# Attention scores from four 64x64 products on the quarters of the array instead of one 128x128 product with two heads on its diagonal

## Chip, core and metric

The kernel runs on one core of one Trainium2 chip. The metric is device time in microseconds (us), the median of several executions; lower is better. The kernel before takes 703.58 us (three runs, 703.25 to 704.31).

A core has five engines that run their own instruction queues in order and wait for each other through semaphores. PE (TensorE) multiplies matrices: a weight load (LDWEIGHTS, listed as PEld) puts the stationary operand, up to 128 rows by 128 columns, into the array, and the matmul streams the moving operand's columns through it into PSUM. DVE (VectorE), ACT (ScalarE) and POOL (GpSimd) do element-wise work, SP issues DMAs.

## The reference

Local attention with summaries, then a feed-forward layer. Batch 4, 8 heads, 768 tokens, head size 64; model width 512, inner width 2048. Each query sees the keys nearer than 16 positions, and 24 summaries of 32 keys each (the maximum over a block's keys; the mean over its values):

```python
k_sum = k.reshape(B, H, nb, block, D).max(axis=3)
v_sum = v.reshape(B, H, nb, block, D).mean(axis=3)
scores_l = scale * np.matmul(q, k.transpose(0, 1, 3, 2))      # kept where |query - key| < 16
scores_s = scale * np.einsum('bhsd,bhnd->bhsn', q, k_sum) + np.log(block)
a = softmax(concatenate([scores_l_m, scores_s]))
x = np.matmul(a, concatenate([v, v_sum]))                     # heads side by side: 3072 x 512
h = x @ w_in
g = np.where(h >= 1, h, np.where(h <= -1, 0.0, (h + 1) ** 2 / 4))
return g @ w_out
```

## The kernel before

**Tiling.** The 3072 tokens are cut in 8 chunks of 384 (half a sequence). A chunk's attention is done for 4 pairs of heads; a pair has 6 query blocks of 64 queries, and each block sees a window of 96 keys plus the 24 summaries: KA = 120 columns. The feed-forward of a chunk has 16 steps of 128 inner columns.

**Attention of one pair.** `scores` (L196) makes the scores: for each query block one fp32 matmul with `q_t[:, blk, :]` as the stationary operand, 128 x 128. It holds the two heads of the pair on its diagonal (head 0 in rows and columns 0 to 63, head 1 in 64 to 127) and zeros elsewhere, so that the product with the 128 x 120 keys (both heads' 64 rows under each other) gives the 64 queries of head 0 in the upper partitions and those of head 1 in the lower ones. Three blocks make one PSUM tile `s_ps`, so a pair has two score tiles, j = 0 for blocks 0 to 2 and j = 1 for blocks 3 to 5. DVE scales and masks a tile into `e` (L204) and takes its maxima `nm` (L208). `exps` (L211) is ACT's exponential, `norms` (L219) divides by the sums (`den`; DVE L221, L222, then POOL L223), `transposes` (L225) turns the probabilities on PE into `t_ps` and ACT copies them to `pt` (L230), `values` (L233) multiplies them with the values: 12 matmuls a pair, each 120 rows by 64 columns, head 0 into the upper and head 1 into the lower half of `o_ps`. `mean_vals` (L191) transposes the summaries of the values.

**Feed-forward.** Weights arrive as float64 words and are split in two halves of fp32r; x and the gated g are split too, so each product is three. `ff1` (L253) is 12 matmuls of 384 columns into `h` (L259; two PSUM buffers), `gate` (L263) makes g on ACT, DVE (L268, L269), ACT and POOL; when L269 has read `h`, its buffer is free for the next `ff1` but one. `ff2` (L276) is 9 matmuls of 512 columns into three accumulators `acc` (L283).

**Weights.** Each of 16 pairs of weight pieces is converted once, during the first chunks, in three steps: `convert_top` (letter a: DVE L101, L103), `convert_low` (b: ACT L110, DVE L111), `convert_split` (c: ACT L116, POOL L117).

**Order.** The program is written as steps of one letter: S scores, E exps, N norms, T transposes, A values, F ff1, G gate, H ff2, a b c conversion. For the first two chunks' attention and the first chunk's feed-forward the order is a table (`FIRST_CHUNK`, L39); from then on one step of the next chunk's attention is put between F and H of each feed-forward step, four such steps to a pair (S E N; values in; T; A). A scheduler in the tile framework may still move independent instructions past each other within an engine's queue. All of an engine's work is one queue in that order. PSUM has six buffers for `s_ps`, `t_ps`, `vs_ps`, `o_ps` and `acc`, and two for `h`.

An fp32 matmul is carried out as two passes, each with its own weight load, so the trace has two MATMUL records for one matmul of the program; the fp32r products of the feed-forward have one.

Of the kernel before, what the change touches and what calls it, by code (L numbers as in the profile page):

```python
# [8 lines left out]
F32 = mybir.dt.float32  # L9
# [31 lines left out]
w2 E011 a0 T000 N011 K03 E010 T001 R02 S020 b0 A00 N010 S021 E020 w1 Z01 T010 E021 R03 N021 N020 T011 A01 a1  # L41
w3 Y02 S030 E030 Z02 S031 a2 T021 T020 E031 N031 Y03 b1 k10 Z03 A02 w5 T031 N030 T030 A03 c0 b2 c2 R10 w4 F00
S100 G00 k11 c1 S101 E101 E100 F01 a3 N101 G01 b3 N100 F02 R11 a4 b4 w6 H00 a5 v10 G02 c3 b5 F03 c4 T100 F04
T101 S111 Z10 w7 A10 F05 a6 H01 G03 S110 G04 b6 c5 w8 H02 w9 E111 v11 E110 a7 N110 T110 k12 Z11 R12 G05 N111
b7 H03 a8 F06 T111 A11 we wa c6 b8 wb G06 H04 H05 F07 c7 a9 b9 c8 aa G07 ba F08 S121 c9 H06 E121 S120 wc v12
F09 F0a ac G08 wd k13 R13 ca bc E120 Z12 H07 H08 N121 G09 N120 ab bb G0a H09 ad bd F0b wf ae cb cd v13 F0c Z13
S131 T120 T121 H0a G0b F0e be ce S130 A12 E130 N130 cc af G0c F0d H0b H0c E131 bf cf T130 N131 F0f T131 G0d
A13 H0d G0f G0e
# [7 lines left out]
def fused_kernel(ctx: ExitStack, tc: tile.TileContext, q2, kT, kwin, vT, vwin, w_in, w_out, mask, ident, out):  # L56
# [12 lines left out]
    mask_sb = const.tile([P, NT + 2, KA], F32, name="mask_sb")  # L69
# [37 lines left out]
    def convert_low(i):  # L107
        # the low word, rounded, gives the last 3 bits and the carry
        w, low = converting[i]
        nc.scalar.mul(out=low, in_=low.bitcast(U32), mul=2.0 ** -29)  # L110
        nc.vector.tensor_tensor(out=w, in0=w, in1=low, op=ALU.add)  # L111
# [19 lines left out]
    # what of the first chunk lies in the weights' rooms  # L131
# [64 lines left out]
    def scores(c, p, j):  # L196
        q_t, k_t = ins[c, p]
        s_ps = ps.tile([P, 512], F32, tag="ps", name=f"s_ps{c}_{p}_{j}")
        for t in range(NT):
            blk = NT * j + t  # L200
            nc.tensor.matmul(s_ps[:, t * KA:(t + 1) * KA], q_t[:, blk, :], k_t[:, blk, :], start=True, stop=True)  # L201
        e = att.tile([P, NT, KA], F32, tag=f"e{j}", name=f"e{c}_{p}_{j}", bufs=E_BUFS)
        at = c % NHALF + j
        nc.vector.scalar_tensor_tensor(  # L204
            out=e, in0=s_ps[:, :NT * KA].rearrange("p (t n) -> p t n", n=KA), scalar=1.0 / math.sqrt(D),
            in1=mask_sb[:, at:at + NT], op0=ALU.mult, op1=ALU.add)
        nm = att.tile([P, NT], F32, tag=f"nm{j}", name=f"nm{c}_{p}_{j}")
        nc.vector.tensor_reduce(out=nm, in_=e, axis=AX.X, op=ALU.max, negate=True)  # L208
        sm[c, p, j] = (e, nm)
# [23 lines left out]
    def values(c, p):  # L233
        v_t = vts[c, p]
        o_ps = ps.tile([P, 512], F32, tag="ps", name=f"o_ps{c}_{p}")
        for blk in range(NB):
            for j in range(2):
# [3 lines left out]
                    pt[c, p, blk // NT][:KA, (blk % NT) * P + j * QB:(blk % NT) * P + (j + 1) * QB],  # L241
# [21 lines left out]
    def gate(c, f):  # L263
        h_ps = hs[c, f]
        # g = max(h, min(t, 1) * t) with t = relu((h + 1) / 2)
# [29 lines left out]
    def load_constants():  # L295
        nc.sync.dma_start(out=mask_sb, in_=mask)
        nc.sync.dma_start(out=ident_sb, in_=ident)
# [101 lines left out]
```

## Time and profile before

| | |
|---|---|
| time, median of three runs | 703.58 us (703.25 to 704.31) |
| span of the profiled execution | 703.5 us, mean granted TensorE clock 0.975 |
| PE busy | 660.8 us (94%), 4064 matmul records |
| PEld busy | 591.2 us (84%) |
| DVE, ACT, POOL busy | 362.4, 336.4, 237.3 us |
| matmuls into h / acc / s_ps / t_ps / o_ps | 1536 / 1152 / 384 / 192 / 768 records |
| DMA | 69.06 MB, mean 98 GB/s |

In the timeline a row is `start us, length us, engine, line, operation, output<-inputs, shape, count`, and after it in brackets the idle time of the engine before it and what ended it. Consecutive like instructions are merged into one row with their count, and its length is then from the first one's start to the last one's end. Matmuls overlap: one's end is modelled some 0.2 us behind the start of the next, so rates are read from starts.

### The profile page before, as it was taken

The page shows a single profiled execution, that of the slowest core. Times are in us where ns is not written, and L with a number is a line of the kernel's source. Part 1 is how long each engine was busy: PE and PEld are TensorE (multiplying, and loading weights), DVE is VectorE, ACT ScalarE, POOL GpSimd, SP SyncE. Part 2 cuts the span into 40 slices and gives each one's busy share as a digit, 9 for nine tenths or more (in the row PEclk, how much of TensorE's full clock was granted, in tenths as well). Part 3 has the DMA queues.
Part 4 walks back from the last instruction along what each step waited for, and adds up shares of the span by engine and source line. Part 5 has one row for each costly group of instructions (what it writes and reads, how often), then busy time and mean ns, then how long its engine had stood idle before and what let it go on. Part 6 is the DMA issues. An engine that isn't in the chain of part 4 may idle for free.

```text
span 703.5 us, 10733 instructions
## 1 busy us (share of the span) xinstructions
PE 660.8 (94%) x4064; PEld 591.2 (84%) x4064; DVE 362.4 (52%) x671; ACT 336.4 (48%) x833; POOL 237.3 (34%) x222
## 2 busy tenths in 40 slices
PE   4858768799999999999999999999999999999997
PEld 3747667689889998989899898989899998989996
DVE  6689999956443444335444554336434443332222
ACT  4777758554444534434444544435444544433222
POOL 1336775752323232223323232223323232222221
PEclk9888988899999999999999999999999999999999
DMA  9999410136111322116212322216212320001001
GB/s 295 370 370 355 151 58 1 48 93 222 61 47 59 129 83 61 61 26 227 65 45 61 121 91 61 55 28 235 62 44 61 106 61 18 1 1 45 1 1 45
DMA packets 31379, 69.06 MB, mean 98 GB/s; under 512 B 2912, under 2 KB 11232, under 8 KB 31328
## 3 DMA queue, kind: packets, MB, share of 16 engines
q1 hardware_dynamic: 31328, 68.38, 29.9%
q8 instruction: 32, 0.52, 0.3%
q14 instruction: 19, 0.16, 0.1%
HBM read 62.07 MB, written 6.29 MB: 97 GB/s over the span
## 4 chain that ended last, share of the span: by engine, by line
PE 82%; DVE 11%; issue 3%; ACT 2%; DMA 1%; SPq 0%; POOL 0%; DVEq 0%; ACTq 0%
PE acc L283 35%; PE h L259 35%; PE s_ps L201 6%; PE o_ps L238 3%; DVE w L103 3%; PE t_ps L228 3%; DVE w L101 2%; DVE w L111 2%; DVE t L268 2%; DMA vraw<-in_vT 1%; DVE t L269 1%; ACT raw L99 1%; DVE e L204 0%; DVE nm L208 0%; PE vs_ps L193 0%
## 5 line engine op out<-in xcount | busy, mean ns | idle before, releaser
L259 PE MATMUL h<-xhi,halves 128*128 128x384 f32 x1024 | 291.6, 346 | 21.6 <-DVE t L269 20.0
L273 POOL TENSOR_TENSOR glo<-t,ghi 128x384 fp32r<-128x384 f32 x128 | 135.3, 1057 | 385.2 <-PE acc L283 187.6
L283 PE MATMUL acc<-halves,ghi 128*128 128x512 f32 x768 | 240.0, 393 | 0.0
L268 DVE SCALAR_TENSOR_TENSOR t<-t 128x384 f32<-128x384 f32 x128 | 87.0, 679 | 277.3 <-ACT t L267 277.0
L259 PEld LDWEIGHTS h<-xhi,halves 128*128 128x128 f32 x1024 | 192.2, 193 | 28.6 <-issue 17.9
L259 PE MATMUL h<-xlo,halves 128*128 128x384 f32 x512 | 175.6, 343 | 0.3 <-DVE xlo L247 0.3
L267 ACT ACTIVATE t<-h,ones_half 128x384 f32<-128x384 f32 x128 | 74.2, 581 | 211.0 <-PE h L259 211.0
L283 PEld LDWEIGHTS acc<-halves,ghi 128*128 128x128 f32 x768 | 145.3, 189 | 27.2
L283 PE MATMUL acc<-halves,glo 128*128 128x512 f32 x384 | 160.5, 418 | 0.7 <-POOL glo L273 0.7
L272 ACT CAST ghi<-t 128x384 fp32r<-128x384 f32 x128 | 65.7, 513 | 110.2 <-DVE t L269 110.1
L259 PEld LDWEIGHTS h<-xlo,halves 128*128 128x128 f32 x512 | 98.7, 193 | 5.4 <-DVE xlo L247 0.7
L283 PEld LDWEIGHTS acc<-halves,glo 128*128 128x128 f32 x384 | 72.8, 190 | 16.6 <-POOL glo L273 1.6
L215 ACT ACTIVATE e<-e,nm 128x120 f32<-128x120 f32 x192 | 73.5, 384 | 11.0 <-DVE nm L208 10.9
L269 DVE TENSOR_TENSOR t<-h,t 128x384 f32<-128x384 f32 x128 | 70.9, 554 | 3.0
L223 POOL TENSOR_TENSOR e<-e,den 128x360 f32<-128x360 f32 x64 | 55.1, 865 | 50.4 <-DVE den L222 36.7
L201 PE MATMUL s_ps<-k,q 128*128 128x120 f32 x360 | 50.2, 291 | 7.2 <-DVE k L163 5.4
L201 PEld LDWEIGHTS s_ps<-k,q 128*128 128x128 f32 x360 | 48.9, 207 | 8.2 <-issue 5.4
L117 POOL TENSOR_TENSOR halves<-w,halves 128x1024 fp32r<-128x1024 f32 x16 | 45.1, 2827 | 15.0 <-ACT halves L116 15.0
L204 DVE SCALAR_TENSOR_TENSOR e<-s_ps,mask_sb 128x360 f32<-128x360 f32 x64 | 33.6, 525 | 5.7 <-PE s_ps L201 5.5
L215 ACT ACTIVATION_READ_ACCUMULATOR e<-e,nm 128x1 f32 x192 | 35.9, 187 | 0.0
L208 DVE TENSOR_REDUCE nm<-e 128x3 f32<-128x360 f32 x64 | 33.4, 522 | 0.8
L238 PEld LDWEIGHTS o_ps<-pt,v 120*64 120x64 f32 x720 | 24.4, 141 | 10.9 <-issue 6.6
(50 smaller groups left out, 408.6 us busy)
## 6 DMA issues: line engine op xcount, KB each, us to landing
q<-in_q SPq DMA_DIRECT2D x30, 384.0 KB, 4.5
k<-in_kwin SPq DMA_DIRECT2D x28, 360.0 KB, 3.5
v<-in_vwin SPq DMA_DIRECT2D x30, 288.0 KB, 2.9
raw<-in_w_in SPq DMA_DIRECT2D x16, 512.0 KB, 9.9
raw<-in_w_out SPq DMA_DIRECT2D x16, 512.0 KB, 10.1
out<-o SPq DMA_DIRECT2D x24, 256.0 KB, 2.1
kraw<-in_kT SPq DMA_DIRECT2D x13, 384.0 KB, 3.8
vraw<-in_vT SPq DMA_DIRECT2D x13, 384.0 KB, 3.5
```

The costliest lines, as they stand in the source:

```text
L117: nc.gpsimd.tensor_tensor(out=halves[:, 1], in0=w.bitcast(F32), in1=halves[:, 0].bitcast(F32), op=ALU.subtract)
L201: nc.tensor.matmul(s_ps[:, t * KA:(t + 1) * KA], q_t[:, blk, :], k_t[:, blk, :], start=True, stop=True)
L215: nc.scalar.activation(out=e[:, t, :], in_=e[:, t, :], func=AF.Exp, bias=nm[:, t:t + 1], scale=1.0, accum_out=den[:, t:t + 1])
L223: nc.gpsimd.tensor_tensor(out=e, in0=e, in1=den.unsqueeze(2).broadcast_to([P, NT, KA]), op=ALU.mult)
L238: nc.tensor.matmul(o_ps[j * D:(j + 1) * D, blk * QB:(blk + 1) * QB], v_t[:KA, blk, j * D:(j + 1) * D], pt[c, p, blk // NT][:KA, (blk % NT) ...
L259: nc.tensor.matmul(h_ps[:, :T], weight["win", f][w][:, k * P:(k + 1) * P], x, start=(n == 0), stop=(n == 3 * NK - 1))
L267: nc.scalar.activation(out=t_sb, in_=h_ps[:, :T], func=AF.Relu, bias=ones_half, scale=0.5)
L268: nc.vector.scalar_tensor_tensor(out=t_sb, in0=t_sb, scalar=1.0, in1=t_sb, op0=ALU.min, op1=ALU.mult)
L269: nc.vector.tensor_tensor(out=t_sb, in0=h_ps[:, :T], in1=t_sb, op=ALU.max)
L272: nc.scalar.copy(out=hi, in_=t_sb)
L273: nc.gpsimd.tensor_tensor(out=lo, in0=t_sb, in1=hi.bitcast(F32), op=ALU.subtract)
L283: nc.tensor.matmul(acc[c][i], a[:, rows], weight["wout", f][w], start=(f == 0 and n == 0), stop=(f == NF - 1 and n == 2))
```

## The change

The scores are made from quarters of the array. For each block and each head a matmul of its own takes 64 rows of q and k (that head's) and 64 columns: the stationary operand is the 64 x 64 block of `q_t` on the diagonal, the moving operand that head's 64 rows of keys. Head j sits in the array's rows 64j to 64j+63; the even block of a couple (i = 0) in columns 0 to 63, the odd one (i = 1) in columns 64 to 127. So four matmuls, two heads by two blocks, cover the four quarters. What is loaded from memory is the same: `q_t` still has its zeros, which are now not read.

A score tile is now one head with all six blocks of the chunk, two blocks above each other, three couples side by side. Both tiles of a pair are made in one step (`S00` in place of `S000` and `S001`), and the table of the first chunks loses the second S of each pair. `values` reads the probabilities of head j from `pt` j. The mask has five kinds of blocks before and four columns of them after, since the upper and the lower partitions take different ones: it comes in by two DMAs of 64 partitions instead of one of 128.

```diff
-    def scores(c, p, j):
+    def scores(c, p):
         q_t, k_t = ins[c, p]
-        s_ps = ps.tile([P, 512], F32, tag="ps", name=f"s_ps{c}_{p}_{j}")
+        s_ps = [ps.tile([P, 512], F32, tag="ps", name=f"s_ps{c}_{p}_{j}") for j in range(2)]
         for t in range(NT):
-            blk = NT * j + t
-            nc.tensor.matmul(s_ps[:, t * KA:(t + 1) * KA], q_t[:, blk, :], k_t[:, blk, :], start=True, stop=True)
+            for j in range(2):
+                rows = slice(j * D, (j + 1) * D)
+                for i in range(2):
+                    blk = 2 * t + i
+                    nc.tensor.matmul(s_ps[j][i * QB:(i + 1) * QB, t * KA:(t + 1) * KA],
+                                     q_t[rows, blk, rows], k_t[rows, blk, :], start=True, stop=True)
...
-        at = c % NHALF + j
+        for j in range(2):
+            at = c % NHALF
...
-                    pt[c, p, blk // NT][:KA, (blk % NT) * P + j * QB:(blk % NT) * P + (j + 1) * QB],
+                    pt[c, p, j][:KA, blk * QB:(blk + 1) * QB],
...
-        nc.sync.dma_start(out=mask_sb, in_=mask)
+        for i in range(2):
+            rows = slice(i * QB, (i + 1) * QB)
+            nc.sync.dma_start(out=mask_sb[rows], in_=mask[rows, i:i + NT + 1])
...
-            do(f"S{c}{p}0 E{c}{p}0 N{c}{p}0 S{c}{p}1 E{c}{p}1 N{c}{p}1")
+            do(f"S{c}{p} E{c}{p}0 N{c}{p}0 E{c}{p}1 N{c}{p}1")
```

The table of the first chunks, its first row as an example:

```diff
-k00 m k01 v00 k02 K01 v01 R00 K00 w0 k03 S000 v02 R01 v03 E000 S001 E001 Y00 N001 N000 Y01 S010 Z00 S011 K02
+k00 m k01 v00 k02 K01 v01 R00 K00 w0 k03 S00 v02 R01 v03 E000 E001 Y00 N001 N000 Y01 S01 Z00 K02 w2 E011 a0
```

Two places of the engines' queues. First PE, at the first scores that lie in the steady alternation of feed-forward and attention (chunk 2, pair 0; in a name like s_ps_0_1 the numbers are the pair and the tile, the last number only tells instances apart; "x3" is three matmuls). Before:

```order
L259 MATMUL h_0_1335<-xhi_3_1306,halves_437 128x384
L201 MATMUL s_ps_0_0_1365<-k_0_1358,q_0_1360 128x120 x3
L201 MATMUL s_ps_0_1_1380<-k_0_1358,q_0_1360 128x120 x3
L283 MATMUL acc_0_557<-halves_1254,glo_14_1332 128x512
L283 MATMUL acc_0_557<-halves_1254,ghi_14_1331 128x512 x2
```

The same place now:

```order
L265 MATMUL h_0_1384<-xhi_3_1355,halves_462 128x384
L205 MATMUL s_ps_0_0_1414<-k_0_1407,q_0_1409 64x120 x2
L205 MATMUL s_ps_0_1_1415<-k_0_1407,q_0_1409 64x120 x2
...
L289 MATMUL acc_0_588<-halves_1303,glo_14_1381 128x512
L289 MATMUL acc_0_588<-halves_1303,ghi_14_1380 128x512 x2
```

Six matmuls have become twelve, in the order head 0 with two blocks, head 1 with two blocks, three times (the rows left out repeat the two above them twice); what stands before and behind them is the same.

Second DVE, where the last weights are converted (t_11 and t_12 are the gates of steps 11 and 12 of the first chunk, e_3 the scores of chunk 1, pair 3, and w the conversions; the gate's second row, which reads h, frees a buffer of h). Before:

```order
L204 SCALAR_TENSOR_TENSOR e_3_1_1119<-s_ps_3_1_1115,mask_sb 128x360
L111 ISA w_1066<-raw_990,w_1066 128x2048
L101 TENSOR_SCALAR w_1088<-raw_823 128x1024
L208 TENSOR_REDUCE nm_3_1_1121<-e_3_1_1119 128x3
L103 SCALAR_TENSOR_TENSOR w_1088<-raw_823,w_1088 128x1024
L268 SCALAR_TENSOR_TENSOR t_11_1144<-t_11_1144 128x384
L111 ISA w_1088<-raw_823,w_1088 128x2048
L269 TENSOR_TENSOR t_11_1144<-h_11_1071,t_11_1144 128x384
L101 TENSOR_SCALAR w_1206<-raw_1084 128x1024
L103 SCALAR_TENSOR_TENSOR w_1206<-raw_1084,w_1206 128x1024
L268 SCALAR_TENSOR_TENSOR t_12_1209<-t_12_1209 128x384
L269 TENSOR_TENSOR t_12_1209<-h_12_1099,t_12_1209 128x384
```

Now:

```order
L274 SCALAR_TENSOR_TENSOR t_11_1201<-t_11_1201 128x384
L100 TENSOR_SCALAR w_1255<-raw_1127 128x1024
L275 TENSOR_TENSOR t_11_1201<-h_11_1114,t_11_1201 128x384
L102 SCALAR_TENSOR_TENSOR w_1255<-raw_1127,w_1255 128x1024
L210 SCALAR_TENSOR_TENSOR e_3_0_1172<-s_ps_3_0_1158,mask_sb 128x360
L210 SCALAR_TENSOR_TENSOR e_3_1_1176<-s_ps_3_1_1159,mask_sb 128x360
L214 TENSOR_REDUCE nm_3_0_1174<-e_3_0_1172 128x3
L214 TENSOR_REDUCE nm_3_1_1178<-e_3_1_1176 128x3
L274 SCALAR_TENSOR_TENSOR t_12_1258<-t_12_1258 128x384
L110 ISA w_1255<-raw_1127,w_1255 128x2048
L227 TENSOR_SCALAR den_3_0_1244<-den_3_0_1244 128x3
L275 TENSOR_TENSOR t_12_1258<-h_12_1142,t_12_1258 128x384
```

Up to the gate of step 10 the queue has done the same set of work in both. One score tile (e and nm) that stood ahead of the gate of step 11 now stands behind it, and the last conversion's L110 (L111 before), which stood behind the gate of step 12, now stands ahead of it, together with the other score tile. On PE the matmuls that make the last two of chunk 1's `s_ps` blocks stood behind the ff1 of step 14 and now stand ahead of it.

More of the change, by code (lines that the diff above doesn't have):

```diff
@@ L39 @@
 FIRST_CHUNK = """
-k00 m k01 v00 k02 K01 v01 R00 K00 w0 k03 S000 v02 R01 v03 E000 S001 E001 Y00 N001 N000 Y01 S010 Z00 S011 K02
[L41 to L48, printed above, removed]
+k00 m k01 v00 k02 K01 v01 R00 K00 w0 k03 S00 v02 R01 v03 E000 E001 Y00 N001 N000 Y01 S01 Z00 K02 w2 E011 a0
+T000 N011 K03 E010 T001 R02 S02 b0 A00 N010 E020 w1 Z01 T010 E021 R03 N021 N020 T011 A01 a1 w3 Y02 S03 E030
+Z02 a2 T021 T020 E031 N031 Y03 b1 k10 Z03 A02 w5 T031 N030 T030 A03 c0 b2 c2 R10 w4 F00 S10 G00 k11 c1 E101
+E100 F01 a3 N101 G01 b3 N100 F02 R11 a4 b4 w6 H00 a5 v10 G02 c3 b5 F03 c4 T100 F04 T101 S11 Z10 w7 A10 F05 a6
+H01 G03 G04 b6 c5 w8 H02 w9 E111 v11 E110 a7 N110 T110 k12 Z11 R12 G05 N111 b7 H03 a8 F06 T111 A11 we wa c6 b8
+wb G06 H04 H05 F07 c7 a9 b9 c8 aa G07 ba F08 S12 c9 H06 E121 wc v12 F09 F0a ac G08 wd k13 R13 ca bc E120 Z12
+H07 H08 N121 G09 N120 ab bb G0a H09 ad bd F0b wf ae cb cd v13 F0c Z13 S13 T120 T121 H0a G0b F0e be ce A12 E130
+N130 cc af G0c F0d H0b H0c E131 bf cf T130 N131 F0f T131 G0d A13 H0d G0f G0e
 """
@@ L67, in fused_kernel @@
     ps = ctx.enter_context(tc.tile_pool(name="ps", bufs=6, space=PSUM))
-    mask_sb = const.tile([P, NT + 2, KA], F32, name="mask_sb")
+    mask_sb = const.tile([P, NT + 1, KA], F32, name="mask_sb")
     ident_sb = const.tile([P, P], F32, name="ident_sb")
@@ L194, in mean_vals @@
         nc.scalar.mul(out=vts[c, p][KW:KA], in_=vs_ps[:NSUM, :P].unsqueeze(1).broadcast_to([NSUM, NB, P]), mul=1.0 / SB)
-    def scores(c, p, j):
+    def scores(c, p):
         q_t, k_t = ins[c, p]
-        s_ps = ps.tile([P, 512], F32, tag="ps", name=f"s_ps{c}_{p}_{j}")
+        s_ps = [ps.tile([P, 512], F32, tag="ps", name=f"s_ps{c}_{p}_{j}") for j in range(2)]
         for t in range(NT):
-            blk = NT * j + t
-            nc.tensor.matmul(s_ps[:, t * KA:(t + 1) * KA], q_t[:, blk, :], k_t[:, blk, :], start=True, stop=True)
-        e = att.tile([P, NT, KA], F32, tag=f"e{j}", name=f"e{c}_{p}_{j}", bufs=E_BUFS)
-        at = c % NHALF + j
[L204 to L209, printed above, removed]
+            for j in range(2):
[5 more added lines that the diff above has]
+        for j in range(2):
+            e = att.tile([P, NT, KA], F32, tag=f"e{j}", name=f"e{c}_{p}_{j}", bufs=E_BUFS)
+            at = c % NHALF
+            nc.vector.scalar_tensor_tensor(
+                out=e, in0=s_ps[j][:, :NT * KA].rearrange("p (t n) -> p t n", n=KA), scalar=1.0 / math.sqrt(D),
+                in1=mask_sb[:, at:at + NT], op0=ALU.mult, op1=ALU.add)
+            nm = att.tile([P, NT], F32, tag=f"nm{j}", name=f"nm{c}_{p}_{j}")
+            nc.vector.tensor_reduce(out=nm, in_=e, axis=AX.X, op=ALU.max, negate=True)
+            sm[c, p, j] = (e, nm)
     def exps(c, p, j):
```

## Prediction

> **What bounds the kernel now.** I read the page first, by slices of 17.6 us:
>
> ```profile
> span 703.5 us, 10733 instructions
> PE   4858768799999999999999999999999999999997
> DVE  6689999956443444335444554336434443332222
> ```
>
> PE is the full engine from the ninth slice on, and DVE before it, from the third to the eighth. The sums over stretches (busy us and instructions of PE, PEld, DVE, ACT, POOL, then clock, DMA share, GB/s) make that exact:
>
> ```profile
> 40.00:60.00 20.00, 14.44 (x83) 12.88 (x80) 19.74 (x25) 15.82 (x31) 9.96 (x7) 0.83 1.05 348
> 120.00:140.00 20.00, 15.38 (x84) 13.58 (x84) 19.85 (x16) 11.72 (x21) 15.44 (x7) 0.77 0.11 31
> 154.00:612.00 458.00, 458.00 (x2935) 413.46 (x2935) 203.09 (x443) 207.12 (x565) 131.12 (x139) 1.00 0.26 81
> ```
>
> From 154 to 612 us PE never pauses, while DVE is busy 44% and ACT 45%: there a microsecond of PE time is a microsecond of the kernel. Until about 134 us DVE is the bound. How many score groups lie in the first stretch tells the row of L201 in that window, with the first and the last group:
>
> ```profile
> L201 PE MATMUL s_ps<-k,q x286: 264/275/275, 154.5 to 611.9; 128*128 128x120 f32 x143
> 154.51 1.49 PE L201 MATMUL s_ps<-k,q 128*128 128x120 f32 x12
> 610.91 1.49 PE L201 MATMUL s_ps<-k,q 128*128 128x120 f32 x12
> ```
>
> 286 records at 12 a group are 24 groups (two records are missing), those of chunks 2 to 7. The eight groups of the first two chunks lie in the part that DVE and the loads bound.
>
> **What a group costs now.** The timeline of PE around one of them:
>
> ```profile
> 312.90 0.33 PE L259 MATMUL h<-xlo,halves 128*128 128x384 f32 x1
> 313.08 0.34 PE L259 MATMUL h<-xhi,halves 128*128 128x384 f32 x1
> 313.25 1.49 PE L201 MATMUL s_ps<-k,q 128*128 128x120 f32 x12
> 314.51 0.48 PE L283 MATMUL acc<-halves,glo 128*128 128x512 f32 x1
> 314.82 0.62 PE L283 MATMUL acc<-halves,ghi 128*128 128x512 f32 x2
> ```
>
> From the start of the last h matmul to that of the second acc matmul pass 1.74 us. An h matmul takes 0.17 (312.90 to 313.08), an acc matmul 0.23 (two in 0.62, of which one alone is 0.39), so the group costs 1.74 - 0.40 = 1.34 us: 12 passes of 0.11. Why 0.11: the transposes stream 128 columns and take the same.
>
> ```profile
> 303.18 0.82 PE L228 MATMUL t_ps<-ident_sb,e 128*120 128x128 f32 x6
> L228 PE MATMUL t_ps<-ident_sb,e 128*120 128x128 f32 x138 | 18.8, 272 | 0.0
> L201 PEld LDWEIGHTS s_ps<-k,q x287: 187/192/192, 154.3 to 611.9; 128*128 128x128 f32 x144
> ```
>
> (0.82 - 0.27) / 5 = 0.109 us for 128 columns makes 0.102 for the 120 of a score pass; that it takes 0.110 I put down to its 128-column weight load (192 ns long, against 138 for the 64-column loads below).
>
> **What 64-column tiles cost.** The kernel already has matmuls on parts of the array: o_ps, 120 rows by 64 columns, left and right half in turn. Their group, its loads, and its first and last pair alone:
>
> ```profile
> 307.86 0.34 PE L259 MATMUL h<-xhi,halves 128*128 128x384 f32 x1
> 308.13 0.92 PE L238 MATMUL o_ps<-pt,v 120*64 120x64 f32 x24
> 308.98 0.50 PE L283 MATMUL acc<-halves,glo 128*128 128x512 f32 x1
> 309.31 0.40 PE L283 MATMUL acc<-halves,ghi 128*128 128x512 f32 x1
> 308.13 0.78 PEld L238 LDWEIGHTS o_ps<-pt,v 120*64 120x64 f32 x24 [0.25 <-issue]
> L238 PEld LDWEIGHTS o_ps<-pt,v x24: 133/138/138, 308.1 to 308.8; 120*64 120x64 f32 x24
> 308.13 0.28 PE L238 MATMUL o_ps<-pt,v 120*64 120x64 f32 x2
> 308.82 0.23 PE L238 MATMUL o_ps<-pt,v 120*64 120x64 f32 x2
> L238 PE MATMUL o_ps<-pt,v 120*64 120x64 f32 x2 | 0.2, 222 | 0.0
> ```
>
> The group costs 309.31 - 307.86 - 0.40 = 1.05 us. The last two passes are 222 ns long each and span 0.23 together, so they start 7 ns apart. The first pair ends at 308.41, the last at 309.05: eleven steps in 0.64, 0.058 a step. A step of two passes thus takes the time that the rate above (0.109 for 128 columns) gives for one pass of 64, 0.055: the two halves work side by side. Twelve steps are 0.70 us; the other 0.35 is paid for going into this mode and out of it (the loads begin only after 0.25 us without any, where those of a score group follow at once).
>
> **The change part by part.** *In the steady stretch.* A group becomes 24 passes of 120 columns on four quarters. If four run side by side, these are 6 steps. A step lies between 0.102 (columns alone) and 0.117 (two 64-column loads of 0.058 in a row); I take 0.105, near the lower end, since half as many columns are loaded. Four starts instead of two add 2 x 7 ns. Sum: 0.35 + 6 x 0.105 + 0.014 = 0.99, against 1.34: 0.35 saved, and between 0.27 (step 0.117) and 0.37 (step 0.102). Times 24: 8.3 us, from 6.5 to 8.8. What two heads on different rows cost side by side no row of this trace shows; o_ps shows it for columns alone. The Trainium skill, page "TensorE: Matmul & The Clock Gate", section "Part 3: Packing small matmuls — row/col tiling", gives 4 ns for each further tile, where my rows have 7; by it the sum would gain another 0.2 us (24 x 3 x 3 ns).
>
> *What hangs on the scores there.* DVE gets the first tile only when nearly the whole group is through, some 0.2 us later than now, and does both tiles one after the other. It has 56% idle, and its result is read by PE two steps, some 10 us, later. The values matmul needs both `pt` from its first product on; they are copied one step ahead of it (end 304.77, use 308.13):
>
> ```profile
> 303.92 0.85 ACT L230 COPY pt<-t_ps 120x384 f32<-120x384 f32 x2
> ```
>
> So 3.4 us of cover; neither costs anything.
>
> *In the first 134 us* the scores' own time is hidden under DVE, but the order moves. Up to the gate of step 10 DVE does the same set of work; then the queue differs. Here PE last waits, and DVE sets it:
>
> ```profile
> 133.25 0.55 DVE L269 TENSOR_TENSOR t<-h,t 128x384 f32<-128x384 f32 x1
> 133.72 0.68 DVE L101 TENSOR_SCALAR w<-raw 128x1024 int32<-128x1024 int32 x1
> 135.57 2.75 DVE L268 SCALAR_TENSOR_TENSOR t<-t 128x384 f32<-128x384 f32 x1
> 138.36 0.56 DVE L269 TENSOR_TENSOR t<-h,t 128x384 f32<-128x384 f32 x1
> 133.94 0.66 PE L259 MATMUL h<-xhi,halves 128*128 128x384 f32 x1 [4.62 <-DVE t L269]
> 137.92 1.04 PE L201 MATMUL s_ps<-k,q 128*128 128x120 f32 x4
> 139.89 0.44 PE L259 MATMUL h<-xhi,halves 128*128 128x384 f32 x1
> 132.12 1.21 DVE L111 CUSTOM_DVE_ANT_0 w<-raw,w 128x2048 uint16<-128x2048 uint16 x1
> 121.82 2.98 DVE L111 CUSTOM_DVE_ANT_0 w<-raw,w 128x2048 uint16<-128x2048 uint16 x1
> ```
>
> The gate of step 11 (133.25) comes 0.3 us earlier (one L101, 0.7, moved ahead of it, one score tile, 1.0, behind it). The gate of step 12 ends at 138.9 now; a score tile (1.0), the last conversion's L111 (1.2) and a `den` (0.1) move ahead of it: 141.2. The ff1 that waits for it starts at 139.89 now, and the 1.0 us of scores ahead of it are gone, so it will wait for the gate: 1.3 us later than now. All else that PE does before it is the same set. So +1.3 us; at worst the moved L111 runs as slowly as the one at 121.82 (+1.8) and the extra issue of the mask delays the queue (0.5 from one SP issue to the next):
>
> ```profile
> 1.64 0.42 SPq L296 DMA_DIRECT2D mask_sb<-in_mask  x1
> 2.11 0.43 SPq L297 DMA_DIRECT2D ident_sb<-in_ident  x1
> DVE e L204 <- PE s_ps L201: 5.5, 5, 2.0
> ```
>
> that is +3.6, say 4. At best the 5.5 us that DVE waits for scores shrink by 2 to 3 us when a pair's scores come in one go: -1.5.
>
> **Sum.** 703.5 - 8.3 + 1.3 = 696.5 us. The span agrees with the median of the runs (703.58) to 0.1, so nothing is added. A difference under 0.2% (1.4 us) could not be told from none.
>
> **The rivals.** *Only two at a time.* All passes stand in one queue, and the two passes of a matmul stand behind each other on the same quarter. If a waiting pass holds up the queue, or the two row halves can't run together, only neighbours overlap: 12 steps. A group then costs 0.35 + 12 x 0.105 + 0.01 = 1.62 instead of 1.34, 24 x 0.28 = 6.7 more: 703.5 + 6.7 + 1.3 = 711.5. It decides at (1.34 - 0.36) / 0.105 = 9 steps a group. For it: the row halves are not seen together in this trace, and o_ps with two tiles needs no more than neighbours. Against it: in o_ps the passes come as twelve pairs, and the first two and the last two start 7 ns apart; a queue held up by each second pass would start with one alone and end with one alone. By the Trainium skill, the same page, section "The mechanism" of Part 3, matmuls start and end strictly in program order, which would make this rival's 711.5; the pairs of o_ps speak against that rule here, but only for column halves. The page's measured packings by rows speak for the forecast. Chance 0.13.
>
> *The loads of the two row halves don't overlap.* Step 0.117, group 1.07, 24 x 0.27 = 6.5 saved: 703.5 - 6.5 + 1.3 = 698.3. For it: only column halves are seen loading together. Against: they do so fully. Chance 0.12.
>
> *The start eats the gain.* The order of the first 134 us would have to lose 7 us or more; the longest single wait of PE there now is about 5 us. The time would be about 703.5, chance 0.07, most of it no difference. That the change doesn't do what it says is hardly possible: the matmuls are of 64 rows and 64 columns with different corners.
>
> **How the numbers follow.** The forecast, four at a time, has 0.68. With the slower loads 0.80 lie faster by over 0.2%; the start's rival gives 0.05 for no difference and 0.02 for slower; with the 0.13 of two at a time slower has 0.15. The range: at best 703.5 - 8.8 - 1.5 = 693.2, and a mode change cheaper by 0.03 makes 692.5; at worst of the faster cases 703.5 - 6.5 + 4 = 701. This leaves out the two slower rivals, 0.2 in all.
>
> **What would show it.** Right: PE's row of 24 score passes is about 0.85 to 0.95 us long, not 1.49, with 0.2 to 0.3 us without loads ahead of it, and the pieces from the last h to the second acc matmul take 1.39 us, not 1.74; the groups, 19.84 us apart now ((610.91 - 154.51) / 23), come 19.5 apart; PE's last long wait is for the gate of step 12 and ends near 141. Wrong: a score row of 1.5 us or longer (two at a time), any wait of PE between 150 and 600 us, or a first stretch that ends after 145.

## The result, and the profile after

The changed kernel takes 708.48 us (median of four executions, 707.64 to 710.16), the kernel before, run beside it, 703.85 us (703.25 to 704.31). The ratio is 1.0073, with a 95% interval of 1.0057 to 1.0088: slower by 0.7%, where 696.5 and thus a faster kernel was forecast. The profiled execution took 708.75 us with a span of 707.0; every run here is some 1.8 us longer than its span, so the execution of before with the span of 703.5 lay nearer to 705.3 than to the median of 703.58.

The slices of the page after, to be held against those of before:

```profile
span 707.0 us, 11468 instructions
PE   2748785599999999999999999999999999999997
DVE  5689999955643343444643444335544443332222
```

PE runs full from the ninth slice on, as before, but the first eight slices are emptier (27487855 against 48587687). The windows, and the first and the last score group of the steady stretch:

```profile
40.00:60.00 20.00, 10.28 (x73) 8.45 (x74) 19.83 (x25) 15.15 (x29) 10.30 (x6) 0.64 1.06 333
120.00:140.00 20.00, 12.77 (x83) 10.73 (x82) 19.80 (x19) 12.07 (x16) 15.51 (x8) 0.93 0.06 21
154.00:612.00 458.00, 457.15 (x3259) 401.11 (x3258) 202.28 (x449) 209.21 (x572) 139.08 (x140) 1.00 0.26 82
165.25 0.85 PE L205 MATMUL s_ps<-k,q 64*64 64x120 f32 x24
614.77 0.84 PE L205 MATMUL s_ps<-k,q 64*64 64x120 f32 x24
```

The last two rows split the result. The first steady group starts at 165.25 instead of 154.51: 10.74 us lost at the start. From the first to the last group pass 449.52 us instead of 456.40: 6.88 gained (7.73 from the groups, less one wait of 0.85 us of PE at 507). Behind the last group stand 92.23 us instead of 92.59: 0.36 gained. Together +3.5, the difference of the spans.

A group of the changed kernel, on PE and on its weight loads, and the first four records of it alone:

```profile
301.47 0.34 PE L265 MATMUL h<-xhi,halves 128*128 128x384 f32 x1
301.74 0.85 PE L205 MATMUL s_ps<-k,q 64*64 64x120 f32 x24
302.51 0.50 PE L289 MATMUL acc<-halves,glo 128*128 128x512 f32 x1
302.85 0.63 PE L289 MATMUL acc<-halves,ghi 128*128 128x512 f32 x2
301.73 0.62 PEld L205 LDWEIGHTS s_ps<-k,q 64*64 64x64 f32 x24 [0.25 <-issue]
301.74 0.33 PE L205 MATMUL s_ps<-k,q 64*64 64x120 f32 x4
```

From the last h matmul to the second acc matmul pass 1.38 us (301.47 to 302.85), where the forecast said 1.39 and before showed 1.74. Four records span 0.33 where one of them is 0.31 long: they start 7 ns apart. The 24 passes are six steps of four, 0.1025 us from step to step.

What PE waited for after the first 60 us, before and after:

```profile
PE h L259 <- DVE t L269: 16.6, 7, 5.1
PE t_ps L228 <- POOL e L223: 2.1, 3, 1.1
```

```profile
PE h L265 <- DVE t L275: 13.4, 4, 5.9
PE t_ps L234 <- ACT v L193: 7.0, 1, 7.0
PE t_ps L234 <- POOL e L229: 2.1, 2, 1.1
PE t_ps L234 <- DVE e L210: 1.4, 1, 1.4
```

A wait of 7.0 us for a transposes' buffer is new. Where it lies, on PE, and what DVE does in that time:

```profile
139.94 0.90 PE L234 MATMUL t_ps<-ident_sb,e 128*120 128x128 f32 x3 [6.97 <-ACT v L193]
143.09 0.90 PE L234 MATMUL t_ps<-ident_sb,e 128*120 128x128 f32 x3 [1.40 <-DVE e L210]
```

```profile
134.84 3.14 DVE L110 CUSTOM_DVE_ANT_0 w<-raw,w 128x2048 uint16<-128x2048 uint16 x1
138.98 0.54 DVE L275 TENSOR_TENSOR t<-h,t 128x384 f32<-128x384 f32 x1
139.45 3.14 DVE L102 SCALAR_TENSOR_TENSOR w<-raw,w 128x1024 int32<-128x1024 int32 x1
142.51 0.96 DVE L210 SCALAR_TENSOR_TENSOR e<-s_ps,mask_sb 128x360 f32<-128x360 f32 x2
145.94 0.54 DVE L275 TENSOR_TENSOR t<-h,t 128x384 f32<-128x384 f32 x1
```

The two L275 rows are the second halves of the gates of steps 11 and 12. They end at 139.5 and 146.5, where they ended at 133.8 and 138.9 before. PE's last wait ends at 143.09, where it ended at 133.94. But the delay is older than this place. These two windows end with the gate of step 10, up to which DVE has done the same 148 instructions in both kernels:

```profile
0.00:120.01 120.01, 85.57 (x499) 73.37 (x500) 105.03 (x148) 82.08 (x172) 60.59 (x49) 0.90 0.69 235
```

```profile
0.00:125.11 125.11, 78.88 (x568) 64.88 (x568) 106.42 (x148) 83.58 (x172) 59.95 (x49) 0.85 0.69 224
```

DVE needs 5.1 us more for them: it is busy 1.4 us longer (106.42 - 105.03) and idle 3.7 us longer (18.7 against 15.0). The groups of these windows show where it idles, before:

```profile
L101 DVE TENSOR_SCALAR w<-raw 128x1024 int32<-128x1024 int32 x14 | 17.9, 1289 | 0.5 <-DMA raw<-in_w_out 0.5
L247 DVE TENSOR_TENSOR xlo<-o_ps,xhi 128x384 fp32r<-128x384 f32 x6 | 3.3, 549 | 0.9 <-ACT xhi L246 0.9
L221 DVE TENSOR_SCALAR den<-den 128x3 f32<-128x3 f32 x14 | 2.4, 190 | 2.6 <-ACT e L215 2.6
```

and after:

```profile
L100 DVE TENSOR_SCALAR w<-raw 128x1024 int32<-128x1024 int32 x14 | 19.2, 1390 | 2.5 <-ACT raw L98 2.4
L253 DVE TENSOR_TENSOR xlo<-o_ps,xhi 128x384 fp32r<-128x384 f32 x6 | 3.3, 548 | 1.8 <-ACT xhi L252 1.8
L227 DVE TENSOR_SCALAR den<-den 128x3 f32<-128x3 f32 x14 | 5.1, 370 | 4.2 <-ACT e L221 4.2
```

The number behind the second bar is DVE's idle time ahead of these instructions: 2.0, 0.9 and 1.6 us more, now all of it waiting for ACT; its other waits are together 0.8 us shorter. Of the busy time, that of one `den` has grown from 0.19 to 0.37 us and that of one L100 from 1.29 to 1.39; other instructions have become shorter, and 1.4 us is what remains. So the steady stretch did what was forecast, and the first 140 us lost more than it gained.

### The profile page after: what moved, and what is told of

Read it like the earlier page. It is cut to its first block, busy times and chain, and to the rows that moved or that the text cites. A ratio compares the mean times of both kernels' runs of the same rounds, so it can differ in the third digit from the quotient of the medians.

```text
span 707.0 us, 11468 instructions
## 1 busy us (share of the span) xinstructions
PE 647.6 (92%) x4448; PEld 564.7 (80%) x4448; DVE 361.0 (51%) x671; ACT 335.9 (48%) x833; POOL 243.3 (34%) x222
## 5 line engine op out<-in xcount | busy, mean ns | idle before, releaser
L274 DVE SCALAR_TENSOR_TENSOR t<-t 128x384 f32<-128x384 f32 x128 | 77.1, 603 | 262.9 <-ACT t L273 261.2
L229 POOL TENSOR_TENSOR e<-e,den 128x360 f32<-128x360 f32 x64 | 61.9, 968 | 71.9 <-DVE den L228 41.3
L275 DVE TENSOR_TENSOR t<-h,t 128x384 f32<-128x384 f32 x128 | 71.0, 556 | 3.8
L116 POOL TENSOR_TENSOR halves<-w,halves 128x1024 fp32r<-128x1024 f32 x16 | 43.5, 2724 | 13.1 <-ACT halves L115 13.0
L234 PE MATMUL t_ps<-ident_sb,e 128*120 128x128 f32 x192 | 30.3, 294 | 17.0 <-POOL e L229 8.7
L234 PEld LDWEIGHTS t_ps<-ident_sb,e 128*120 128x120 f32 x192 | 24.3, 147 | 21.1 <-POOL e L229 10.7
L205 PE MATMUL s_ps<-k,q 64*64 64x120 f32 x720 | 28.2, 283 | 10.9 <-DMA q<-in_q 6.0
L205 PEld LDWEIGHTS s_ps<-k,q 64*64 64x64 f32 x720 | 20.6, 140 | 18.5 <-issue 17.8
```

The costliest lines, as they stand in the source:

```text
L116: nc.gpsimd.tensor_tensor(out=halves[:, 1], in0=w.bitcast(F32), in1=halves[:, 0].bitcast(F32), op=ALU.subtract)
L205: nc.tensor.matmul(s_ps[j][i * QB:(i + 1) * QB, t * KA:(t + 1) * KA], q_t[rows, blk, rows], k_t[rows, blk, :], start=True, stop=True)
L229: nc.gpsimd.tensor_tensor(out=e, in0=e, in1=den.unsqueeze(2).broadcast_to([P, NT, KA]), op=ALU.mult)
L234: nc.tensor.transpose(t_ps[:KA, t * P:(t + 1) * P], sm[c, p, j][0][:, t, :], ident_sb)
L274: nc.vector.scalar_tensor_tensor(out=t_sb, in0=t_sb, scalar=1.0, in1=t_sb, op0=ALU.min, op1=ALU.mult)
L275: nc.vector.tensor_tensor(out=t_sb, in0=h_ps[:, :T], in1=t_sb, op=ALU.max)
```

## Experiments

The theory after the first reading: the start loses because the scores of a pair, made in one step, put the queues in a poorer order. The rivals: a full set of PSUM buffers, and the mask that comes in by two DMAs.

**e1_old_start.** Quarters everywhere, but in the first two chunks one head a step, from the table of before.

```diff
-    def scores(c, p):
+    def scores(c, p, *heads):
+        heads = heads or (0, 1)
...
-            for j in range(2):
+            for j in heads:
...
```

> Quarters everywhere and one head to a score tile, but in the first two chunks the two tiles of a pair are made in two steps at the places where they stood before the change (one head a step, two quarters at a time); from chunk 2 on all four quarters in one step. Theory A (the order of the first two chunks, two score tiles at once, lost the time): the start is as before, the first steady score group at 154 to 156 us, and the steady 24 x 0.36 = 8.7 us are kept: 694 to 697 us. Theory B (the quarters themselves are what slows the start: mode changes, more instructions): first steady group at 160 us or later, 700 us or more.

Measured: 698.63 us (697.57 to 700.59) against 704.27 of the kernel before, ratio 0.9925 (0.9901 to 0.9949). With the steps of the start back in their old order, the change is a gain: the first steady group starts at 155.5 us, as the theory had it, but the time lies 1.6 us above the range that the theory gave.

**e2_order_only.** The 128 x 128 products and the one mask DMA of before, with both tiles of a pair made in one step, from the table after.

```diff
+        for j in range(2):
+            products(c, p, j)
+        for j in range(2):
+            masked(c, p, j)
...
```

> The score products of before (128 x 128 with two heads on the diagonal, three blocks a tile), but both tiles of a pair in one step, in the table of the changed kernel. Theory A: the start loses as much as in the changed kernel, about 10 us, the first steady score group begins at 162 to 167 us, nothing is saved later: 711 to 716 us. Theory B: the start is as before, 704 us.

Measured: 706.4 us (705.31 to 707.27), ratio 1.0031 (1.0021 to 1.0042). That is neither number of the expectation: making both tiles in one step costs some 2 us by itself, and the start of the change loses five times that. Its profiled execution has the span of that of before, 703.5, and the same start of the steady groups, 154.51, so the two traces don't show where the 2 us of the medians lie.

**e3_last_pair_later.** The change, with the scores of chunk 1, pair 3 moved behind the transposes of pair 2, so that PE's 7 us wait for a buffer goes.

```diff
-F0c Z13 S13 T120 T121 H0a G0b F0e be ce A12 E130
+F0c Z13 T120 T121 H0a G0b F0e be ce S13 A12 E130
```

> The changed kernel with one step of its table moved: the scores of chunk 1, pair 3 stand behind the transposes of pair 2 and just ahead of the values of pair 2, instead of ahead of those transposes. Theory A1 (the two score tiles held PSUM buffers that the transposes waited 7.0 and 1.4 us for, and the gates behind them slipped): these waits go, the first steady score group comes at 158 to 162 us instead of 165, and the time is 701 to 705 us. Rival A2 (DVE's own delay sets the end of the start, the PSUM wait only lies in front of it): at most 1 us better, 707 to 709 us.

Measured: 709.09 us (708.3 to 710.13), ratio 1.0069 (1.0052 to 1.0086): nothing gained, as the rival of its expectation had it. What PE waits for from 60 to 170 us:

```profile
PE h L258 <- DVE t L268: 20.8, 6, 5.9
PE t_ps L227 <- POOL e L222: 2.0, 2, 1.0
```

The wait for the buffer is gone, and the waits for DVE's gates have grown from 13.4 to 20.8. The full buffers only showed a DVE that was late anyway.

**e4_one_mask_dma.** The change, with the mask's rows laid out for it beforehand in memory and loaded by one DMA.

```diff
-        for i in range(2):
-            rows = slice(i * QB, (i + 1) * QB)
-            nc.sync.dma_start(out=mask_sb[rows], in_=mask[rows, i:i + NT + 1])
+        nc.sync.dma_start(out=mask_sb, in_=mask)
...
```

> The changed kernel with its mask laid out on the host so that it comes in by one DMA of 128 partitions instead of two of 64. If the additional issue on SP (about 0.6 us, everything behind it later) delays the start, the first score group starts 0.5 us earlier and the time is 0.5 to 1.5 us lower, about 707 us; if the loads are bound by the DMA engines anyway, no difference: 708.5 us.

Measured: 699.92 us (699.41 to 701.13), ratio 0.994 (0.9925 to 0.9955). One DMA in place of two, 8.6 us. That was not expected by any theory, and it made a new one: that DMAs of 64 partitions slow the loads of the start. From 10 to 20 us the change moved 314 GB/s, the kernel before 350 and this one 349.

**e5_old_start_one_mask.** e1 with the mask of e4.

```diff
...
-            nc.sync.dma_start(out=mask_sb[rows], in_=mask[rows, i:i + NT + 1])
+        nc.sync.dma_start(out=mask_sb, in_=mask)
...
```

> This is e1_old_start (products on the quarters, first two chunks one head a step as before the change) with its mask laid out beforehand for the quarters and loaded by one DMA of 128 partitions. Theory, that the two DMAs of 64 partitions slow the loads of the start and that nothing else of the start is lost once the old order is back: the 24 steady groups give 24 x 0.36 = 8.7 us, so 704.3 - 8.7 = 695.6 us, from 694.5 to 697, that is 3 us below e1_old_start. Rival, that the mask's two DMAs cost as much here as between the change and e4_one_mask_dma (8.5 us): 690. Second rival, that they cost only in the new order: 698.6, as e1_old_start.

Measured: 696.1 us (695.86 to 696.62) against 704.18, ratio 0.9893 (0.9879 to 0.9908). The number is the one that the theory of the slow loads gave, but e6 and e7 below refute that theory, so here it was right by luck. The 8.1 us gained come near to the 24 x 0.36 = 8.7 of the groups. Its groups:

```profile
153.01 0.84 PE L207 MATMUL s_ps<-k,q 64*64 64x120 f32 x24
601.80 0.85 PE L207 MATMUL s_ps<-k,q 64*64 64x120 f32 x24
```

They lie 19.51 us apart (448.79 / 23), against 19.84 before, and begin 1.5 us earlier than before. So the two traces, whose spans differ by 9.4 us, have 7.6 of it from the first to the last group, 1.5 ahead of them and 0.3 behind. This is the fastest version here.

**e6_before_split_mask.** The kernel before with its mask by two DMAs of 64 rows.

```diff
-        nc.sync.dma_start(out=mask_sb, in_=mask)
+        for i in range(2):
+            rows = slice(i * QB, (i + 1) * QB)
+            nc.sync.dma_start(out=mask_sb[rows], in_=mask[rows])
```

> The kernel before, with its mask loaded by two DMAs, rows 0 to 63 and rows 64 to 127, and nothing else changed. Theory, that two DMAs of 64 partitions slow the loads of the start by themselves: slower by 3 us (what e1_old_start lacks of 704.3 - 8.7) up to 8.5 us, so 707 to 713, with less than 3.2 MB moved from 10 to 20 us, where the kernel before moves 3.5. Rival, that the split costs only together with the new order or with the products on the quarters: 704 to 705 and 3.5 MB.

Measured: 708.76 us (706.67 to 709.84), ratio 1.0067 (1.0052 to 1.0083). The split costs 4.6 us in a kernel that is otherwise unchanged. But the second half of the expectation failed: from 10 to 20 us it moved 349 GB/s, as much as without the split.

**e7_mask_by_columns.** e4 with two DMAs of all 128 partitions, each half of the columns.

```diff
-        nc.sync.dma_start(out=mask_sb, in_=mask)
+        for i in range(2):
+            cols = slice(2 * i, 2 * i + 2)
+            nc.sync.dma_start(out=mask_sb[:, cols], in_=mask[:, cols])
```

> The change with its mask laid out beforehand and loaded by two DMAs, but each of all 128 partitions and half of the columns, so that the number of DMAs is that of the change. If it is the 64 partitions that spoil the loads: as e4_one_mask_dma, 699 to 701 us, 3.4 MB or more from 10 to 20 us. If it is one DMA more ahead of the others, whatever its form: as the change, 707 to 709, 3.2 MB or less.

Measured: 700.37 us (699.58 to 701.2), ratio 0.9951 (0.9939 to 0.9963), so it is not the number of DMAs. The time is as expected for the 64 partitions, but the 3.4 MB that belonged to it are not there. Its rates from 10 to 20 us (the last column), and below them those of e6:

```profile
10.00:20.00 10.00, 5.72 (x67) 3.96 (x69) 6.81 (x21) 5.71 (x25) 3.18 (x4) 1.00 1.06 290
```

```profile
10.00:20.00 10.00, 6.02 (x47) 5.28 (x49) 7.35 (x23) 5.31 (x22) 1.99 (x3) 1.00 1.05 349
```

In those 10 us e7 loads more slowly than any other of these kernels and is 8 us faster than the change, and e6, with loads as fast as before, is 4.6 us slower than before. The rate of the loads doesn't decide the time, and the theory of the slow loads fell with these two rows.

**e8_head_by_head.** e4 with the two loops of the products exchanged, so that a pair's head 0 stands whole ahead of head 1 in PE's queue.

```diff
-        for t in range(NT):
-            for j in range(2):
+        for j in range(2):
+            for t in range(NT):
```

> e4_one_mask_dma with the loops of the score products exchanged: all six products of one head (rows 0 to 63 of the array), then all six of the other (rows 64 to 127), so that neighbours in the queue lie on the two column halves of one row half. If in the change all four quarters run side by side, a group now takes 12 steps of 0.1025 us and not 6, and the time rises by 24 x 6 x 0.1025 = 14.8 us to about 714.7. If only two quarters ever run at once, or the queue takes the heads apart by itself, nothing changes: 699 to 701.

Measured: 703.18 us (701.25 to 705.45), ratio 0.9989 (0.9975 to 1.0003), which is neither number. A group of it, and the first and the last group:

```profile
290.81 0.34 PE L265 MATMUL h<-xhi,halves 128*128 128x384 f32 x1
291.08 1.10 PE L205 MATMUL s_ps<-k,q 64*64 64x120 f32 x24
292.11 0.50 PE L289 MATMUL acc<-halves,glo 128*128 128x512 f32 x1
292.44 0.63 PE L289 MATMUL acc<-halves,ghi 128*128 128x512 f32 x2
...
152.68 1.10 PE L205 MATMUL s_ps<-k,q 64*64 64x120 f32 x24
607.42 1.10 PE L205 MATMUL s_ps<-k,q 64*64 64x120 f32 x24
```

A group costs 1.63 us (290.81 to 292.44), 0.25 more than 1.38: some two and a half steps more, not six. The starts of its records come in pairs, one chain at 291.08, .23, .33, .44, .54 and .64, and a second at 291.35, .50, .60, .71, .81 and .91: the second head begins 0.27 us behind the first and then runs beside it. (Records 13 ns apart, at 291.334 and 291.347, can't share a quarter, whose step is 0.1025.) So the quarters do run side by side, and the queue let a later matmul start on free rows while earlier ones still stood in line for theirs. Why it did so only after 0.27 us isn't shown. The groups lie 19.77 us apart (454.74 / 23), against 19.51 in e5: 0.26 x 24 = 6.2 us. A faster start hides part of that: the first steady group begins 4.8 us earlier than e4's (157.49), though nothing in the exchange should make the start faster.

**What the queues show.** That last point leads to the order of the built programs. In the start most of these kernels stand in different orders on every engine, also where their steps are written in the same order. VectorE from its sixth row on, in the change:

```
6 L162 COPY k_0_94<-kraw_0_92 128x6x16
7 L210 SCALAR_TENSOR_TENSOR e_0_0_143<-s_ps_0_0_129,mask_sb 128x360
8 L210 SCALAR_TENSOR_TENSOR e_0_1_147<-s_ps_0_1_130,mask_sb 128x360
9 L214 TENSOR_REDUCE nm_0_0_145<-e_0_0_143 128x3
10 L214 TENSOR_REDUCE nm_0_1_149<-e_0_1_147 128x3
11 L168 TENSOR_REDUCE ks_1_153<-first_88 128x24
```

and in e4, which differs by the mask's DMA alone:

```
6 L162 COPY k_0_94<-kraw_0_92 128x6x16
7 L168 TENSOR_REDUCE ks_1_152<-first_88 128x24
8 L210 SCALAR_TENSOR_TENSOR e_0_0_142<-s_ps_0_0_128,mask_sb 128x360
9 L210 SCALAR_TENSOR_TENSOR e_0_1_146<-s_ps_0_1_129,mask_sb 128x360
10 L214 TENSOR_REDUCE nm_0_0_144<-e_0_0_142 128x3
11 L214 TENSOR_REDUCE nm_0_1_148<-e_0_1_146 128x3
```

With two DMAs the scheduler puts the first pair's masked scores ahead of the next pair's key summaries. Compared place by place, 106 of DVE's 671 rows, 99 of ACT's 640, 16 of POOL's 222 and 175 of PE's 3680 differ, those of DVE all within its first 171. Between the kernel before and e6 it is 80, 63, 12 and 116; between e4 and e7 none; between e4 and e8 199 of DVE's. (The expectations below have 135, 7 and 3 rows of DVE where the places are 106, 11 and 4.) So the theories became two: the *form* of the loads, or the *order* that the scheduler made on account of them. Four kernels tell them apart.

**e9_mask_first_rows** and **e10_mask_first_one.** The mask's loads issued ahead of the first keys, by two DMAs of 64 partitions and by one of 128. The four engines have the same order in both.

```diff
-k00 m k01 v00 k02 K01 v01 ...
+m k00 k01 v00 k02 K01 v01 ...
...
```

> The order of the built program shows that the one DMA of e4_one_mask_dma also put other instructions of the start in another order on every engine (135 of 671 VectorE rows), as the split did in e6_before_split_mask. So there are two theories for the 8.5 us. Form: two DMAs of 64 partitions slow the loads themselves. Order: the DMA only moves the time that the scheduler reckons with, and the other order of the start costs the time. This kernel is the change with the mask's two DMAs of 64 partitions issued ahead of the first keys; its built order is that of e10_mask_first_one, row for row on the four engines, so the two differ in the form of the load alone. Form: 4 to 8 us slower than e10. Order: within 1.5 us of e10.

> As e9_mask_first_rows, with one DMA of 128 partitions for the mask. Form: 4 to 8 us faster than e9. Order: within 1.5 us of e9. The time itself neither theory gives, since this order has not run (between 694 and 710).

Measured: e9 700.88 us (698.86 to 703.62), ratio 0.9962 (0.9949 to 0.9976); e10 701.29 us (698.3 to 701.95), ratio 0.9951 (0.9933 to 0.9969). In one order the form of the loads makes no difference: 0.4 us, and not to the side that the form theory needs.

**e11_change_order_one_mask.** e4 with the identity by two DMAs of 64 rows, which gives the order of the change (but for 11 places of DVE and 2 of ACT) with one DMA for the mask.

```diff
-        nc.sync.dma_start(out=ident_sb, in_=ident)
+        nc.sync.dma_start(out=ident_sb[:64], in_=ident[:64])
+        nc.sync.dma_start(out=ident_sb[64:], in_=ident[64:])
```

> The mask by one DMA as in e4_one_mask_dma, and the identity by two DMAs of 64 rows, by which the scheduler arrives at the order of the change again (7 of 671 VectorE rows and 2 of ScalarE stand elsewhere, none of TensorE or GpSimd). Order: as the change, 707 to 710. Form, if it is the mask's two loads: 699 to 701, as e4.

Measured: 707.97 us (706.82 to 709.75), ratio 1.006 (1.0046 to 1.0075), as the change. Its waits of PE from 60 us on and its first steady group:

```profile
PE h L265 <- DVE t L275: 12.6, 4, 5.2
PE t_ps L234 <- ACT v L193: 7.0, 1, 7.0
...
PE t_ps L234 <- DVE e L210: 1.4, 1, 1.4
```

```profile
165.34 0.84 PE L205 MATMUL s_ps<-k,q 64*64 64x120 f32 x24
```

The same waits of 7.0 and 1.4 us as in the change, and the same start of the steady stretch within 0.1 us. With the order came the time. Since e11 has two loads of 64 rows itself, those of the identity, it takes e9 and e12 to rule such loads out.

**e12_before_other_order.** The kernel before with its mask by four DMAs of 128 partitions, which gives the order of e6 (but for 4 places of DVE and 2 of POOL).

```diff
-        nc.sync.dma_start(out=mask_sb, in_=mask)
+        nc.sync.dma_start(out=mask_sb[:, 0:1], in_=mask[:, 0:1])
+        nc.sync.dma_start(out=mask_sb[:, 1:2], in_=mask[:, 1:2])
+        nc.sync.dma_start(out=mask_sb[:, 2:3], in_=mask[:, 2:3])
+        nc.sync.dma_start(out=mask_sb[:, 3:5], in_=mask[:, 3:5])
```

> The kernel before with its mask by four DMAs of all 128 partitions, by columns. The scheduler then arrives at the order of e6_before_split_mask (3 of 671 VectorE rows and 2 of GpSimd stand elsewhere), with no DMA of 64 partitions. Order: as e6, 707 to 710. Form: as the kernel before, 703 to 705.5.

Measured: 710.0 us (708.28 to 710.53) against 703.46, ratio 1.008 (1.0066 to 1.0095). The slow order without any load of 64 partitions is as slow as with them (708.76).

The kernels of one order stand together in this table. Its third column is the time at which DVE ends the gate of step 10. Those with 128 x 128 products (the kernel before, e6, e12) gain nothing behind the start.

| kernel | mask | gate of step 10 ends at | first steady group at | time, us |
|---|---|---|---|---|
| the change | two, by rows | 125.11 | 165.25 | 708.48 |
| e11, order of the change | one (identity: two, by rows) | 125.32 | 165.34 | 707.97 |
| e4 | one | 120.63 | 157.49 | 699.92 |
| e7, order of e4 | two, by columns | 120.68 | 156.99 | 700.37 |
| e9 | two, by rows | 121.46 | 157.78 | 700.88 |
| e10, order of e9 | one | 122.49 | 158.98 | 701.29 |
| before | one | 119.97 | 154.51 | 703.46 to 704.27 |
| e6, another order | two, by rows | 124.29 | 158.29 | 708.76 |
| e12, order of e6 | four, by columns | 125.34 | 159.30 | 710.0 |
| e5, table of before | one | 117.64 | 153.01 | 696.1 |

The time goes with the order and not with the form of the loads: two kernels of one order lie 0.4 to 1.2 us apart, the change and e4 8.6. PE's granted clock, a rival that no kernel was made for, doesn't separate these two either: its mean over the first 60 us is 0.79 in the change and 0.80 in e4 (0.89 before). In e5 it is 0.97, and what of e5's early start comes with the clock is open.

The Trainium skill, page "DMA: Bandwidth & Descriptors", section "Rules for kernel authors", says that two transfers to the two halves of the partitions gain nothing over one of 128, since both run on all sixteen DMA engines. e9 and e10 agree: 700.88 and 701.29.

## Why the prediction was wrong

**The steady stretch: right.** The sum was 0.35 + 6 x 0.105 + 0.014 = 0.99 us for a group and 0.35 us saved; the trace has 1.38 against 1.74, 0.36 saved. The step is 0.1025, inside the bounds 0.102 to 0.117. From group to group it is a little less, 0.33 us in e5 (19.84 to 19.51), and 24 groups then give 7.9 to 8.7 us (8.3 forecast); e5 is 8.1 us faster, though its start has a share in that. What hangs on the scores there cost nothing, but for the one wait of 0.85 us. That the span agreed with the median, so that nothing was added to the sum, was chance: an execution is 1.8 us longer than its span.

***Only two at a time* and *the loads of the two row halves don't overlap*: excluded.** The first needs a row of 1.5 us or more, the second a step of 0.117; the row is 0.85 and the step 0.1025. The rule behind the first is that of the Trainium skill, page "TensorE: Matmul & The Clock Gate", section "The mechanism" of Part 3: matmuls start and end strictly in the order of the program. In e8 the second head's first record starts at 291.35, ahead of the first head's fourth step at 291.44, so the trace disagrees for tiles on different rows, where the measurement decides.

**The start: this step failed.** The prediction put +1.3 us, at worst +4, and the trace has +10.7 to the first steady group. It took "Up to the gate of step 10 DVE does the same set of work; then the queue differs" to mean that DVE also takes the same time for it, and priced the moved rows at the two gates behind. The gate of step 10 ends 5.1 us later with the same 148 instructions. From the gate of step 11 to that of step 12 DVE needs 7.0 us, where the working gives 7.7 (from 133.5 to 141.2): that part of the working was right to 0.7 us, and the part that was taken as unchanged was not. Three parts make the 10.7:

- 5.1 us up to the gate of step 10: 3.7 of DVE's idling (more for ACT's exponentials, for ACT's first conversion step and for `xhi`, less elsewhere), 1.4 of DVE's instructions being longer.
- 4.1 us from there to the end of PE's last wait (143.09 - 133.94 = 9.15 in all). It was forecast as a wait for the gate of step 12 that ends near 141; it is a wait for PSUM buffers behind the same DVE queue. By e3 the gates take its place when it is removed.
- 1.6 us more from that wait to the first steady group (22.16 against 20.57). PE never pauses in either, and in the change seven more acc matmuls lie there (34 against 27, at 0.23 us each), work that it had not got done earlier.

**The mask's second DMA: wrong in kind.** It had 0.5 us in the worst case, the price of its issue. Its issue costs nothing that can be seen (e7 against e4, 700.37 and 699.92); the scheduler turned the order of all engines round on account of it, and that is 8.6 us between the change and e4. Of the 10.7 us to the first steady group, 7.8 go with this order (165.25 against 157.49); e4 keeps the other 3.0. Why the scheduler did it isn't shown; that it reckons with when loads arrive is likely. A row's price can't show such a thing. The orders of the two programs, compared from their first row and not from the gate of step 10, would have shown that they differ, though not what it costs.

***The start eats the gain*: this is what happened**, with 0.07 for it and 703.5 as its time, which was still 5 us too low. Its condition, a loss of 7 us or more, was set against the longest single wait of PE (5.1). That was no bound: the loss is spread over several waits of DVE, the longest of 4.0 us, and over longer instructions. Of the signs of being wrong, a wait of PE in the steady stretch did come, but it was 0.85 us and not the cause.

Shown by experiments is that the order makes the loss (e4, e7, e9 to e12), that no buffer and no rate of loads makes it (e3, e6, e7), and that the quarters gain about what was forecast in a start that ends as early as before (e5, whose order is not that of before: 195 of DVE's places differ). That DVE is late with the slow orders already at the gate of step 10 shows in all the kernels of the table (124.3 to 125.3 against 117.6 to 122.5); that idling and longer instructions make it late is read from two traces. Which of the moved rows starts it was not tried, nor where e2 has its 2 us. e1 and e5 differ by 2.5 us with 19 of DVE's places in another order; for these the form was not taken apart from the order.

## What to carry to other kernels

Where a scheduler decides the order, any edit, even of a constant's load at the start, may turn the order of all engines in a stage that waits often. Here that was worth 8.6 us in the changed kernel and 4.6 to 6.5 in the one before, while e7's second DMA moved nothing. So compare the whole order of the two programs, not only the part that the edit names. The same set of work need not take the same time in another order on an engine that waits: here the same 148 instructions took 5.1 us longer. Before blaming a transfer for a loss, make the pair of kernels that has the same order with two forms of the transfer, and the pair that has two orders with the same form.

## What the runs showed of the hardware

Four fp32 products on the quarters of the array ran side by side: 7 ns from start to start, one step of four in 0.1025 us, which is what 120 columns take alone by the rate of the transposes (0.109 for 128); the weight loads, 133 ns each, added nothing to it. A group of 24 still paid 0.35 us for going in and out (1.38 less 0.40, six steps and 0.02 for the starts), as the group of `o_ps` did. In e8 the second row half began 0.27 us behind the first, when three of the first's six steps, all ahead of it in the queue, had still to start.

The time of the start went with the order to about a microsecond: the first steady groups of two kernels of one order lie 0.1 us (the change and e11), 0.5 (e4 and e7), 1.0 (e6 and e12) and 1.2 (e9 and e10) apart. And DVE's instructions were far from constant in the start. The sixteen conversions' L110 (shortest, median and longest in ns), and POOL at the long one of 134.84:

```profile
L110 DVE CUSTOM_DVE_ANT_0 w<-raw,w x16: 1207/1214/3305, 24.8 to 144.7; 128x2048 uint16<-128x2048 uint16 x16
```

```profile
130.77 6.14 POOL L116 TENSOR_TENSOR halves<-w,halves 128x1024 fp32r<-128x1024 f32 x2
```

It took 3.14 us, and POOL's L116 ran beside it up to 136.9. The other two of more than 3 us (104.52 and 126.64) also had POOL's L116 beside them, for 2.1 and 2.2 us; those that no POOL instruction met took 1.21 to 1.23. No run here takes POOL's work away, so that POOL is the cause isn't shown. Which of DVE's instructions meets POOL changes with the order.
